# The end of a two-branch spectral kernel: last rows sent through DRAM, eight products without a reader, three pools with one buffer more, and a rewritten order

## The chip, the cores and the metric

The kernel runs on one core of a Trainium2 chip. The metric is device time in microseconds: the median of several executions, 537.49 us before the change. One more execution was profiled, and all durations below come from it.

## The reference

The input `x` is a float32 array of 2048 rows (positions) by 640 columns (channels). Two branches are computed from it and mixed by a gate per row:

```
g = sigmoid((x * gate_w).sum(-1))                      # one number per row
a: K[d, l] = 2 Re sum_n C[d, n] exp(A[d, n] dt[d] l)   # 128 complex modes per channel
   y = irfft(rfft(x, 4096) * rfft(K, 4096))[:2048] + x * D_skip
b: y = irfft2(rfft2(x) * (w_r + 1j * w_i))
out = g * a + (1 - g) * b
```

Branch a is a causal convolution along the 2048 positions with a generated filter K. Branch b is a filter in the two-dimensional spectrum.

## The kernel before

Everything is float32 except the arguments of the exponentials, which are split into bfloat16 parts. A Fourier transform of length 4096 is done as two stages of matrix products (`stage1`, 64x128 outputs, and `stage2`, 64x160 outputs) with tables that come in as inputs. The 640 channels are worked in four chunks of 160, called `c`, and the 4096 frequencies in 17 pairs of blocks, gathered in groups that start at block pair `g0`.

The program has these parts:

- `phase_p` prepares the parameters of the modes. `phase_a`, first half, transforms `x` and writes its spectrum to DRAM (`u_d`). `phase_b` generates the filter K: exponentials and sines on ScalarE (`e`, `sc`), their products on VectorE and GpSimd (`x`, `y`), outer products on TensorE (`p_k`, L745), result to DRAM (`k_d`).
- `phase_a`, second half, is branch b: for each of nine block pairs it folds the spectrum (`fo`, `fg`), transposes it on TensorE (`p_t`), copies that to `ft` on ScalarE (L555), multiplies with tables (`p_d`, L566 and L567), filters on VectorE (`mm`, `zz`, `pm`, `ff`), transposes back (`p_t`, copied to `pmt`, L553), multiplies again (`p_eo`, L611 and L612) and writes `s3e_d` to DRAM. `ft` and `pmt` have one buffer each (pools `f_t` and `f_p`). This half runs interleaved with `phase_b`.
- `phase_c` and `phase_d` finish branch a. For each chunk: `stage1` and `stage2` on the filter (L367, L380), product with the stored spectrum `us` on VectorE (`ma` L856, `mb` L857) and sums on VectorE and GpSimd (`t2`, L862), inverse `stage2` (`p_i`, L886), a copy on ScalarE (`s3`, L888), and a write of `s3` to DRAM (`s3_d`, L898). `us` comes from pool `c_u`, three buffers, loaded on ScalarE's DMA queue (L843).
- The end of `phase_d` mixes: `last_e` multiplies the rows of branch b (`t3e`, product `p_e`, L172) and scales them with the gate (`oe`, L944); `last_c` does the same for branch a (`t3`, product `p_c`, L960), scales (L965) and adds (L966), or both in one instruction for the last chunk (L963). Each is called for two halves of eight rows (`a`), in three pieces of 3, 3 and 2 rows. `p_e` and `p_c` share a pool of two PSUM buffers.

The last chunk, c = 3, takes its groups in the order g0 = 0, 4, 8, 16, 12. `t3` of this chunk collects 64 rows from `s3` of groups 0, 4, 8 and 12. Groups 0, 4 and 8 go through DRAM like all others. Group 12 is the last work of the inverse transform; its rows go straight from `s3` to `t3` inside SBUF, by eight DMAs of 80 KB, four issued by SyncE (SP) and four by ScalarE (ACT), each into four partitions of `t3` (L896).

The order of all instructions on all five engines is written out as numbers: a table `ORDER` of index ranges per engine, and a table `CROSS` of extra edges between engines for buffers, put on the traced instructions by `arrange`.

Of the kernel before, what the change touches and what calls it, by code (L numbers as in the profile page):

```python
# [384 lines left out]
def phase_a(tc, A, T):  # L385
    nc = tc.nc
# [96 lines left out]
    with ExitStack() as ctx:  # L483
# [4 lines left out]
        wu, wo, wg, ac, wt, w3p, wb = pool("f_u", 1), pool("f_o", 1), pool("f_g", 1), pool("f_c", 1), pool("f_t", 1), pool("f_3", 2), pool("f_b", 1)  # L488
        wp, ww, w4, wk = pool("f_p", 1), pool("f_w", 1), pool("f_4", 3), pool("f_k", 2)
# [297 lines left out]
def phase_c(tc, A, T, ctx):  # L787
# [8 lines left out]
    T.kp, T.cc, T.up = pool("c_k", 2), pool("c_c", 1), pool("c_u", 3)  # L796
# [30 lines left out]
def phase_d(tc, A, T, ctx, out):  # L827
# [45 lines left out]
    def backs(c, g0, gn, st):  # L873
        t2 = st.t2
        if c == 3 and g0 in (4, 12):
            s3 = T.kp.tile([128, 20, 64], F32, tag="k", name="s3").rearrange("p q a -> p (q a)").rearrange("p (x d) -> p x d", d=160)
        else:
            s3 = w2k.tile([128, 8 if gn > 1 else 1, 160], F32, tag="s3%d" % min(2, gn), name="s3")
        np_ = gn * st.nl // 64
        k0 = 2 * g0  # L880
        for h in range(0, np_, 4):
# [9 lines left out]
            if k0 == 32:  # L891
                nc.scalar.dma_start(T.s3_d[c, 33], s3[0:64, 0, :])
            elif (c, g0) == (3, 12):
                t3 = t3s[3].rearrange("p x a d -> p (x a) d")
                for i in range(h, h + 4):
                    (nc.scalar if i % 2 else nc.sync).dma_start(t3[16 * i + 3:16 * i + 16:4], s3[:, i, :])  # L896
            elif h:
                nc.scalar.dma_start(T.s3_d[c, 2 * k0:2 * (k0 + h) + 8].rearrange("(x k) a d -> (k a) x d", k=2), s3[:, 0:h + 4, :])  # L898
# [28 lines left out]
    def load_c(c, p, n, eng=nc.sync):  # L927

        if p == 0 and c != 2:
            t3s[c] = dk.tile([128, 2, 16, 160], F32, tag="t3", name="t3")  # L930
        elif p == 0:
            t3s[c] = T.tp[0].tile([128, 32, 160], F32, tag="t1", name="t3").rearrange("p (x a) d -> p x a d", x=2)
        for y in range(p // 16, (p + n) // 16):
            src = T.s3_d[c, 16 * y:16 * y + 16].rearrange("k (j x a) d -> (k j) x a d", x=2, j=2)
            eng.dma_start(t3s[c][y::4], src)
# [77 lines left out]
    load_c(3, 32, 16, eng=nc.scalar)  # L1013
    run(last_c(2, 0))
    run(last_c(2, AG))
    for dst, ot in held:
# [121 lines left out]
```

## Time and profile before

| | |
|---|---|
| median of 3 runs | 537.49 us (534.48 to 539.0) |
| the profiled execution | 538.59 us |
| its span, first to last instruction | 536.8 us |
| mean granted TensorE clock | 0.975 |
| busy: TensorE | 496.7 us (93%) |
| busy: VectorE | 429.3 us (80%) |
| busy: ScalarE | 309.5 us (58%) |
| busy: GpSimd | 276.3 us (51%) |
| DMA | 99.89 MB, mean 186 GB/s |

TensorE is PE in the profile (matmuls) and PEld (weight loads), VectorE is DVE, ScalarE ACT, GpSimd POOL, SyncE SP. A float32 product shows as two matmuls in the trace, so eight products are 16 of its rows. "Clock" is the share of full speed that TensorE was granted. The 1.8 us between the profiled time and its span lie around the program.

### The profile page before, as it was taken

What the parts mean: (1) busy time and instruction counts of PE and PEld (TensorE: products, weight loads), DVE (VectorE), ACT (ScalarE), POOL (GpSimd) and SP (SyncE); (2) the same over time, 40 slices, a digit from 0 to 9 for tenths busy, and PEclk for the clock granted to TensorE, in tenths of its full rate; (3) what the DMA queues carried; (4) which work ended last, traced back from release to release, by engine and by line L of the source; (5) the groups of instructions that cost most, each with busy time, mean ns of one, the idle gap of its engine ahead of it and who ended that gap; (6) DMA issues with size and microseconds to landing.
All of it is one profiled execution on the core that took longest, in us unless ns stands there. A gap on an engine that the chain in (4) does not pass through costs nothing. (4 is left out here: it accounts for less than half of the span.)

```text
span 536.8 us, 17117 instructions
## 1 busy us (share of the span) xinstructions
PE 496.7 (93%) x7432; PEld 382.1 (71%) x7432; DVE 429.3 (80%) x644; ACT 309.5 (58%) x469; POOL 276.3 (51%) x285
## 2 busy tenths in 40 slices
PE   8889999989899999999999999889989999998945
PEld 6889976757566767767767676558958889987611
DVE  3699867887989999988979779553986987979933
ACT  4667065698686876876986977876313333341200
POOL 4596415466438275257264255163733666638740
PEclk9979999999879999999999999999999999999987
DMA  8927760582160433170512231284849799899962
GB/s 333 406 95 272 250 237 18 208 270 89 52 217 2 127 104 93 33 263 6 142 37 84 74 123 57 74 313 146 318 139 376 263 363 341 275 295 295 324 227 101
DMA packets 47666, 99.89 MB, mean 186 GB/s; under 512 B 3588, under 2 KB 33048, under 8 KB 45928
## 3 DMA queue, kind: packets, MB, share of 16 engines
q1 hardware_dynamic: 25544, 67.08, 36.3%
q10 hardware_dynamic: 19552, 22.19, 12.8%
q0 software_dynamic: 2496, 9.54, 5.2%
q8 instruction: 58, 0.95, 0.7%
q14 instruction: 16, 0.13, 0.1%
HBM read 59.47 MB, written 38.99 MB: 183 GB/s over the span
## 5 line engine op out<-in xcount | busy, mean ns | idle before, releaser
L380 PE MATMUL p_s<-t,w 128*64 128x160 f32 x1056 | 89.2, 307 | 4.4 <-ACT ut L415 3.6
L380 PEld LDWEIGHTS p_s<-t,w 128*64 128x64 f32 x1056 | 76.2, 135 | 13.0 <-ACT ut L415 4.2
L731 POOL TENSOR_TENSOR y<-e,sc 128x512 f32<-128x512 f32 x40 | 52.5, 1315 | 38.3 <-ACT sc L712 37.3
L706 PE MATMUL p_p<-rp,par 64*128 64x512 bf16 x480 | 62.6, 381 | 7.5 <-DVE x L728 6.2
L697 ACT ACTIVATE e<-p_e 128x1024 f32<-128x1024 f32 (+1 forms) x80 | 62.0, 815 | 8.7 <-PE p_e L696 7.5
L732 POOL TENSOR_TENSOR y<-e,sc 128x512 f32<-128x512 f32 x40 | 52.8, 1319 | 18.4 <-ACT sc L712 18.3
L718 ACT ACTIVATE p_p<-p_p 128x1024 f32<-128x1024 f32 x40 | 40.5, 1012 | 24.2 <-PE p_p L706 19.9
L368 ACT COPY t<-p_s 128x512 f32<-128x512 f32 x40 | 25.1, 628 | 46.8 <-PE p_s L367 41.1
L726 DVE SCALAR_TENSOR_TENSOR x<-e,p_p 128x512 f32<-128x512 f32 x40 | 27.3, 682 | 26.9 <-ACT p_p L718 26.9
L728 DVE TENSOR_TENSOR x<-e,p_p 128x1024 f32<-128x1024 f32 x40 | 48.5, 1213 | 0.0
L745 PEld LDWEIGHTS p_k<-x,y 128*32 128x32 f32 x2560 | 38.5, 111 | 14.0 <-issue 11.4
L888 ACT COPY s<-p_i 128x640 f32<-128x640 f32 x32 | 22.1, 693 | 43.9 <-PE p_i L886 36.7
L745 PE MATMUL p_k<-x,y 128*32 128x64 f32 x2560 | 44.7, 223 | 1.2 <-DVE x L728 0.5
L712 ACT ACTIVATE sc<-p_p 128x1024 f32<-128x1024 f32 x40 | 40.9, 1023 | 7.8 <-PE p_p L706 7.5
L862 POOL TENSOR_TENSOR t<-ma 64x320 f32<-64x320 f32 x32 | 29.4, 918 | 31.2 <-DVE ma L856 29.4
L886 PE MATMUL p_i<-t,w 128*64 128x160 f32 x528 | 42.6, 300 | 2.1 <-DVE mb L857 2.1
L706 PEld LDWEIGHTS <-par 64*128 64x128 bf16 x480 | 20.2, 94 | 33.0 <-issue 11.1
L367 PE MATMUL p_s<-c,kt 128*64 128x128 f32 x640 | 42.9, 273 | 0.0
L886 PEld LDWEIGHTS p_i<-t,w 128*64 128x64 f32 x528 | 37.3, 137 | 6.2 <-POOL t L862 1.6
L367 PE MATMUL p_s<-c,u 128*64 128x128 f32 x640 | 40.3, 283 | 1.0 <-DMA c<-in_t_c 1.0
L367 PEld LDWEIGHTS p_s<-c,u 128*64 128x64 f32 x640 | 37.5, 142 | 4.0 <-issue 3.4
L367 PEld LDWEIGHTS p_s<-c,kt 128*64 128x64 f32 x640 | 38.4, 136 | 1.6 <-POOL kt L807 0.4
(163 smaller groups left out, 1071.5 us busy)
## 6 DMA issues: line engine op xcount, KB each, us to landing
u_d<-ut SPq DMA_DIRECT2D x32, 320.0 KB
us<-u_d ACTq DMA_DIRECT2D x16, 640.0 KB
s_d<-s ACTq DMA_DIRECT2D x15, 640.0 KB
t<-s_d SPq DMA_DIRECT2D x14, 640.0 KB
ww<-in_w_l SPq DMA_DIRECT2D x8, 642.0 KB
ue<-u_d SPq DMA_DIRECT2D x8, 640.0 KB
k_d<-kt SPq DMA_DIRECT2D x4, 1280.0 KB
kt<-k_d SPq DMA_DIRECT2D x8, 640.0 KB
```

Of the source, the lines that this page charges most:

```text
L367: nc.tensor.matmul(p[64 * ri:64 * ri + 64, j, :], src(i + j), e1[ri], start=True, stop=True)
L380: ins = nc.tensor.matmul(p[64 * j:64 * j + 64, i, 160 * ri:160 * ri + 160], w2[:, x, 64 * ri:64 * ri + 64], t1[:, x // 2 if x < 32 else K0 ...
L697: st.exp = S.activation(ef[:, :, c:c + n], p[:, :, 0:n], AF.Exp)
L706: P.matmul(p[:, j, 0:n], pars[0][t][x], w[x, y:y + n], start=i == 0, stop=i == 2)
L712: S.activation(sc.rearrange("p d v i -> p (d v i)"), p.rearrange("p j w -> p (j w)"), AF.Sin, scale=TWO_PI)
L718: T.trig = st.trig = S.activation(f, f, AF.Sin, scale=TWO_PI)
L728: V.tensor_tensor(out=x[:, 0].rearrange("p d (h j) -> p d h j", h=2), in0=e[:, :, 0:64].rearrange("p d (h j) -> p d h j", h=2), in1=cx.uns ...
L731: G.tensor_tensor(out=y[:, 1], in0=e[:, :, 64:96], in1=sc[:, 0], op=ALU.mult)
L732: G.tensor_tensor(out=y[:, 0], in0=e[:, :, 64:96], in1=sc[:, 1], op=ALU.mult)
L745: P.matmul(st.pb[32 * r:32 * r + 32, o, :], y[:, ri, 4 * qq + JR[r], :], x[:, ri, 4 * qq + JR[r], :], start=t % 2 + qq + 1 - ri == 0, stop ...
L862: return eng.tensor_tensor(out=t2[64 * im:64 * im + 64, o, :], in0=m[l, :hn, 0, :], in1=m[l, :hn, 1, :], op=ALU.add if im else ALU.subtract)
L886: T.mm = P.matmul(p[x:x + 64, i // 2, 160 * (i % 2):160 * (i % 2) + 160], T.w3[:, k0 + h + i, x:x + 64], t2[:, h + i, :], start=True, stop ...
```

## The change

It has five parts.

1. Group 12 of the last chunk is written to `s3_d` like the others, in two DMAs of 320 KB on ACT, one after each copy of `s3`. Two new DMAs of 320 KB on SP read it back into `t3`, each for eight of 16 rows per partition (`load_c(3, 48, 16, 2)`). The eight 80 KB DMAs inside SBUF are gone.
2. Eight products of `s3` with itself (128x128 weights, 480 columns) go into a PSUM tile that nobody reads.
3. Pools `f_t` and `f_p` get two buffers.
4. Pool `c_u` gets four buffers.
5. The tables `ORDER` and `CROSS` are rewritten for all five engines.

The diff without the tables:

```
-        ... pool("f_t", 1), pool("f_3", 2), pool("f_b", 1)
-        wp, ww, w4, wk = pool("f_p", 1), ...
+        ... pool("f_t", 2), pool("f_3", 2), pool("f_b", 1)
+        wp, ww, w4, wk = pool("f_p", 2), ...
...
-    T.kp, T.cc, T.up = pool("c_k", 2), pool("c_c", 1), pool("c_u", 3)
+    T.kp, T.cc, T.up = pool("c_k", 2), pool("c_c", 1), pool("c_u", 4)
...
+        T.s3 = s3
...
-            elif (c, g0) == (3, 12):
-                t3 = t3s[3].rearrange("p x a d -> p (x a) d")
-                for i in range(h, h + 4):
-                    (nc.scalar if i % 2 else nc.sync).dma_start(t3[16 * i + 3:16 * i + 16:4], s3[:, i, :])
-            elif h:
-                nc.scalar.dma_start(T.s3_d[c, 2 * k0:2 * (k0 + h) + 8]..., s3[:, 0:h + 4, :])
+            elif h or (c, g0) == (3, 12):
+                x = h if (c, g0) == (3, 12) else 0
+                T.sd = nc.scalar.dma_start(T.s3_d[c, 2 * (k0 + x):2 * (k0 + h) + 8]..., s3[:, x:h + 4, :])
...
-    def load_c(c, p, n, eng=nc.sync):
+    def load_c(c, p, n, parts=1, eng=nc.sync):
...
+        w = 16 // parts
         for y in range(p // 16, (p + n) // 16):
             src = T.s3_d[c, 16 * y:16 * y + 16].rearrange("k (j x a) d -> (k j) x a d", x=2, j=2)
-            eng.dma_start(t3s[c][y::4], src)
+            for a in range(0, 16, w):
+                T.ld = eng.dma_start(t3s[c][y::4, :, a:a + w], src[:, :, a:a + w])
...
     load_c(3, 32, 16, eng=nc.scalar)
+    load_c(3, 48, 16, 2)
     run(last_c(2, 0))
     run(last_c(2, AG))
+    p = ps.tile([128, 2, 512], F32, tag="ps", name="p_w2")
+    for _ in range(8):
+        P.matmul(p[:, 0, 0:480], T.s3[:, 4, 0:128], T.s3[:, 5:8, :], start=True, stop=True)
     for dst, ot in held:
         nc.sync.dma_start(dst, ot[:, :, :])
```

What the tables decide at the program's end is best seen in the order itself. On TensorE, before, from the first inverse product of group 12 (`p_i_7044`) to the end of the program; `t_6810` is `t3` of chunk 2 and `t_6893` that of chunk 3:

```order
L886 MATMUL p_i_7044<-t_7002,w_5241 64x160 x8
L172 MATMUL p_e<-t3e,c_66 64x480 x4
L172 MATMUL p_e<-t3e,c_66 64x320 x2
L886 MATMUL p_i_7058<-t_7002,w_5241 64x160 x8
L960 MATMUL p_c<-t_6810,c_66 64x480 x4
L960 MATMUL p_c<-t_6810,c_66 64x320 x2
L960 MATMUL p_c<-t_6810,c_66 64x480 x4
L960 MATMUL p_c<-t_6810,c_66 64x320 x2
L960 MATMUL p_c<-t_6893,c_66 64x480 x4
```

On TensorE after the change, the same stretch (lines have moved by a few numbers; L1019 are the eight new products):

```order
L887 MATMUL p_i_7044<-t_7002,w_5241 64x160 x8
L172 MATMUL p_e<-t3e,c_66 64x480 x2
L172 MATMUL p_e<-t3e,c_66 64x320 x2
L887 MATMUL p_i_7055<-t_7002,w_5241 64x160 x8
L172 MATMUL p_e<-t3e,c_66 64x480 x4
L1019 MATMUL p_w_7101<-s_7043 128x480 x8
L172 MATMUL p_e<-t3e,c_66 64x320 x2
L960 MATMUL p_c<-t_6810,c_66 64x480 x4
L960 MATMUL p_c<-t_6810,c_66 64x320 x2
L960 MATMUL p_c<-t_6810,c_66 64x480 x4
L960 MATMUL p_c<-t_6810,c_66 64x320 x2
L960 MATMUL p_c<-t_6893,c_66 64x480 x4
```

The second half of `p_e` has moved behind the last inverse product, and the eight new products stand between its pieces, ahead of all `p_c` of chunks 2 and 3.

On ACT before, from the copy and write of group 16 (`s_7037`) to the end; `s_7043` is group 12:

```order
L890 COPY s_7037<-p_i_7038 128x160
L892 DMA s_d<-s_7037 64x160
L888 COPY s_7043<-p_i_7044 128x640
L896 DMA t_6893<-s_7043 4x32x160 x2
L935 DMA t_6893<-s_d 32x5120
L888 COPY s_7043<-p_i_7058 128x640
L896 DMA t_6893<-s_7043 4x32x160 x2
```

On ACT after, the same stretch:

```order
L891 COPY s_7037<-p_i_7038 128x160
L889 COPY s_7043<-p_i_7044 128x640
L896 DMA s_d<-s_7043 128x4x160
L893 DMA s_d<-s_7037 64x160
L889 COPY s_7043<-p_i_7055 128x640
L896 DMA s_d<-s_7043 128x4x160
L935 DMA t_6893<-s_d 32x5120
```

The load of rows 32 to 47 of `t3` (L935), which waits for the write of group 16, stood ahead of the second copy and now stands behind it.

On SP before, the last DMAs:

```order
L935 DMA t_6893<-s_d 32x5120 x2
L896 DMA t_6893<-s_7043 4x32x160 x4
L1017 DMA out<-ot 128x1280 x2
L971 DMA out<-ot 128x1280
L971 DMA out<-ot 128x960
```

On SP after:

```order
L935 DMA t_6893<-s_d 32x5120 x2
L935 DMA t_6893<-s_d 32x2x1280 x2
L1021 DMA out<-ot 128x1280 x2
L971 DMA out<-ot 128x1280
L971 DMA out<-ot 128x960
```

The two reads of group 12 stand where the four DMAs inside SBUF stood, ahead of the outputs of chunk 2.

More of the change, by code (lines that the diff above doesn't have):

```diff
@@ L485, in pool @@
             return ctx.enter_context(tc.tile_pool(name=name, side="right", reuse_waits="tile", bufs=bufs))
-        wu, wo, wg, ac, wt, w3p, wb = pool("f_u", 1), pool("f_o", 1), pool("f_g", 1), pool("f_c", 1), pool("f_t", 1), pool("f_3", 2), pool("f_b", 1)
-        wp, ww, w4, wk = pool("f_p", 1), pool("f_w", 1), pool("f_4", 3), pool("f_k", 2)
+        wu, wo, wg, ac, wt, w3p, wb = pool("f_u", 1), pool("f_o", 1), pool("f_g", 1), pool("f_c", 1), pool("f_t", 2), pool("f_3", 2), pool("f_b", 1)
+        wp, ww, w4, wk = pool("f_p", 2), pool("f_w", 1), pool("f_4", 3), pool("f_k", 2)
         ps = ctx.enter_context(tc.tile_pool(name="f_ps", side="right", reuse_waits="tile", bufs=3, space=PSUM))
@@ L1041 @@
     "PE": """
[22 rows of a table removed]
[23 rows of a table added]
 """,
     "DVE": """
[12 rows of a table removed]
[12 rows of a table added]
 """,
     "Activation": """
[10 rows of a table removed]
[10 rows of a table added]
 """,
     "Pool": """
[5 rows of a table removed]
[6 rows of a table added]
 """,
     "SP": """
[3 rows of a table removed]
+1+3 8+3 0 4+2 11 6+2 15+2 12 14 13 26 17+9 27 37 28+9 38+8 58 61 47 46 57 48+2 59 50+3 62 53+3 60 65 56 63 69 67 74 66 71 64 72 79 70 85 76 68 77 75
+81 90 83 73 82 80 87 78 88 95 86 92 84 93 91 89 97+3 96 94 100+2 106 108 107 102 104 103 105 109 112 111 113 110 116 115 114 118 117 124 122 120+2 119
+125 123 127 126 128+9
 """,
@@ L1111 @@
 P259>V591 P259>V595 P259>V596 P263>V601 P263>V602 P263>V606 P263>V607 P267>V612 P67>V169 P67>V174 P81>V208 P81>V210 P93>V241 P93>V243 S118>A477
-S118>A478 S119>A487 S119>A488 S119>A490 S119>A491 S119>A492 V143>P63 V143>P64 V143>P66 V147>P71 V147>P72 V147>P74 V161>P67 V167>P86 V167>P87 V167>P89
-V194>P81 V203>P100 V203>P101 V203>P103 V224>P93 V236>P109 V236>P110 V236>P112 V263>P108 V269>P127 V269>P128 V269>P130 V296>P122 V305>P141 V305>P142
-V305>P144 V329>P136 V338>P150 V338>P151 V338>P153 V365>P149 V398>P163 V427>P172 V485>P206 V485>P207 V485>P208 V485>P209 V529>P233 V529>P234 V529>P235
-V529>P236 V576>P259 V576>P260 V576>P261 V576>P262 V612>P272 V612>P273 V612>P274 V612>P275
+S118>A478 S119>A490 V143>P63 V143>P64 V143>P66 V147>P71 V147>P72 V147>P74 V161>P67 V167>P86 V167>P87 V167>P89 V194>P81 V203>P100 V203>P101 V203>P103
+V224>P93 V236>P109 V236>P110 V236>P112 V263>P108 V269>P127 V269>P128 V269>P130 V296>P122 V305>P141 V305>P142 V305>P144 V329>P136 V338>P150 V338>P151
+V338>P153 V365>P149 V398>P163 V427>P172 V485>P206 V485>P207 V485>P208 V485>P209 V529>P233 V529>P234 V529>P235 V529>P236 V576>P259 V576>P260 V576>P261
+V576>P262 V612>P272 V612>P273 V612>P274 V612>P275
 """
```

2 lines of the change are left out of this document (1 added, 1 removed), and 103 rows, old and new, of the table ORDER.

## The prediction

> **What bounds the kernel now.** I read the page first: busy shares and slices.
>
> ```profile
> PE 496.7 (93%) x7432; PEld 382.1 (71%) x7432; DVE 429.3 (80%) x644; ACT 309.5 (58%) x469; POOL 276.3 (51%) x285
> PE   8889999989899999999999999889989999998945
> PEclk9979999999879999999999999999999999999987
> ```
>
> TensorE is busy in nearly every slice, with VectorE close behind; only the last two slices (510 to 537 us) fall to 4 and 5 tenths, and there the granted clock falls too. So a change can win in two places: small waits spread over the first 510 us, or the end. The spread part comes from a table of stretches (columns: length, then busy time and count of each engine, clock, DMA share, GB/s):
>
> ```profile
> 125.00:150.00 25.00, 21.22 (x364) 14.89 (x365) 22.74 (x32) 17.85 (x24) 13.04 (x13) 0.89 0.25 79
> 275.00:300.00 25.00, 24.95 (x345) 18.17 (x342) 24.86 (x38) 18.16 (x28) 14.78 (x15) 1.00 0.22 66
> 450.00:475.00 25.00, 25.00 (x361) 23.99 (x358) 22.84 (x35) 9.86 (x16) 14.00 (x16) 1.00 0.87 285
> 100.00:375.00 275.00, 261.63 (x4028) 186.80 (x4028) 229.72 (x342) 214.48 (x313) 136.88 (x141) 0.98 0.36 117
> ```
>
> Between 100 and 375 us TensorE idles 13.4 of 275 us; the worst stretch, 125 to 150, has 3.8 of them and a clock of 0.89. In the next two rows nothing is left. There is little to win before the end.
>
> The end, first TensorE's own timeline, then the chain that ended last:
>
> ```profile
> 509.98 1.26 PE L886 MATMUL p_i<-t,w 128*64 128x160 f32 x16
> 511.06 5.09 PE L960 MATMUL p_c<-t,c 128*64 128x480 f32 x24
> 524.62 6.80 PE L960 MATMUL p_c<-t,c 128*64 128x480 f32 x20 [8.47 <-DMA out<-ot]
> ...
> 518.64 5.75 DMA out<-ot
> ```
>
> The last inverse product ends at 511.24. The mix of chunk 2 follows until 516.15, then TensorE stands still for 8.47 us. The profile names an output DMA as what ended the wait, but `p_c` of chunk 3 reads `t3`, not `ot`. What it can wait for is the last rows' DMAs:
>
> ```profile
> 512.16 0.53 ACTq L935 DMA_DIRECT2D t<-s_d  x1
> 512.74 0.69 ACT L888 COPY s<-p_i 128x640 f32<-128x640 f32 x1 [4.90 <-DMA s_d<-s]
> 513.46 1.51 ACTq L896 DMA_DIRECT2D t<-s  x2
> 516.23 2.76 SPq L1017 DMA_DIRECT2D out<-ot  x2
> ...
> 518.00:520.00 2.00, 0.00 (x0) 0.00 (x0) 0.00 (x0) 0.00 (x0) 0.62 (x1) 0.94 0.80 287
> 522.00:524.00 2.00, 0.00 (x0) 0.00 (x0) 0.00 (x0) 0.00 (x0) 0.00 (x0) 0.50 0.24 95
> 528.00:530.00 2.00, 1.92 (x8) 0.44 (x6) 1.64 (x5) 0.00 (x0) 0.00 (x0) 0.50 0.00 0
> ```
>
> ACT's second copy of group 12 could have run at 511.5, but stood 4.90 us behind the load L935, which waited for group 16's write. The small DMAs went out only at 513.46, and their data moved beside two outputs until 524, in the end at 95 GB/s with a quarter of the DMA engines at work. The clock column shows the rest of the damage: with TensorE empty it fell just before 520 and still stood at 0.50 up to 530, so nearly all of chunk 3's products ran at half clock.
>
> **The change part by part.** All sums are against the profiled execution: span 536.8 us, 538.59 with what lies around it, which is 1.10 above the median of 537.49.
>
> *Last rows through DRAM.* The copy no longer waits behind L935, and its write is issued about 1 us after the last inverse product (0.69 for the copy and the steps to it). The two DRAM steps are not in this trace in this form. The nearest rows:
>
> ```profile
> s3e_d<-s POOLq DMA_DIRECT2D x4, 320.0 KB, 2.8
> par<-par_d POOLq DMA_DIRECT2D x8, 160.0 KB, 2.9
> ...
> 382.45 8.89 DMA t3e<-s3e_d
> 397.82 10.23 DMA s_d<-s
> ```
>
> From below, a 320 KB write at 2.8 and a read at 2.9 make 5.7 us. From above, a 640 KB write and a 1280 KB read in the crowded start of the last phase make 10.23 + 8.89 = 19.1 us. The new transfers are small, and the outputs of chunk 2 are now queued behind them on SP instead of running beside them, so I stay near the lower end and take 8 us: `t3` is whole 9 us after the last inverse product.
>
> What TensorE has to do meanwhile, from the same point: the second half of `p_e`, which used to stand ahead of it, the eight products, then `p_c` of chunk 2.
>
> *Eight products.* Each is two passes of 480 columns with 128x128 weights. Two rows of full-width float32 products bound a pass:
>
> ```profile
> 1.44 3.41 PE L411 MATMUL p_w<-lg 128*128 128x512 f32 x4 [1.44 <-DVE lg L406]
> 1.00:4.30 3.30, 2.86 (x4) 1.17 (x4) 0.56 (x2) 1.28 (x1) 1.78 (x3) 1.00 0.74 230
> ...
> 339.74 1.08 PE p_i L626 x4
> 450.18 0.81 PE p_e L172 x4
> ```
>
> From above, the first four passes of the program: 0.85 for 512 columns, 0.80 for 480, so 12.8 us for 16. From below, L626 in the middle of the program: 0.27 for 320 columns, 0.40 for 480, so 16 x 0.40 = **6.4 us**. I take this one: the same width, float32, in steady work. (The last row, narrow products two side by side, gives 0.20 a pass, 3.2 us, but a full-width pass cannot share the array.)
>
> The Trainium skill speaks to the upper row: its page "TensorE: Matmul & The Clock Gate", section "Part 1: The HAM clock gate", says that TensorE begins at half rate and is released after about 3.4 us of work. By that rule the first row is a half-clock price, and 0.40 is right from both sides; the clock column shows 1.00 there, and by it the sum would be 6.4 us worse.
>
> The eight wait for the second copy, 0.9 us after the last inverse product; `p_e` covers that. So from there: `p_e` of half a chunk 2.2 us (two pieces of 0.81, one of two thirds of it), 6.4, then 5.1 for `p_c` of chunk 2. That is 13.7 us, and the data were there at 9. **Chunk 3 starts on TensorE's time, not on the DMA's.** The wait of 8.47 us goes, and 6.4 us of products stand in its place, in front of all that is left, so they cost their full length. The `p_e` moved behind is no cost, since it is missing ahead; VectorE's `oe` (L944) moves with it and runs beside the eight products.
>
> *The clock.* TensorE no longer stops, so chunk 3 runs at full clock. Before:
>
> ```profile
> 528.13 1.74 DVE L963 SCALAR_TENSOR_TENSOR ot<-p_c,gate,oe 128x160 f32<-128x160 f32 x5 [0.63 <-PE p_c L960]
> 530.66 2.59 DVE L963 SCALAR_TENSOR_TENSOR ot<-p_c,gate,oe 128x160 f32<-128x160 f32 x8 [0.79 <-PE p_c L960]
> 516.72 0.84 DVE L966 TENSOR_TENSOR ot<-ot,oe 128x320 f32<-128x320 f32 x1
> ```
>
> From 524.62 to the last L963 at 533.25 it took 8.63 us. At full clock VectorE sets the pace: a first product of 0.81, sixteen L963 of 2.59/8 = 0.32 (5.2 us), some 0.5 of seams, and about half of chunk 2's last add (0.84), which now stands directly ahead: 6.9 to 7.3. Gain **1.5 us**.
>
> *Buffers and order.* One buffer each for `ft` and `pmt` cost TensorE 0.3 and 0.7 us:
>
> ```profile
> PE p_eo L611 <- ACT pmt L553: 0.7, 1, 0.7
> PE p_d L566 <- ACT ft L555: 0.3, 1, 0.3
> DVE ma L856 <- issue: 6.3, 6, 3.4
> 391.39 2.55 PE L172 MATMUL p_e<-t3e,c 128*64 128x480 f32 x12 [2.39 <-DMA t3e<-s3e_d]
> ```
>
> Two buffers can give that 1.0 back. The third row includes VectorE's waits for `us`; most of it lies where TensorE is full, so a fourth buffer brings nothing I can name, and its earlier loads run beside reads that TensorE waits for, such as `t3e` in the last row. From -1.0 to +2.4, I take -0.5 for all of it: both waits sit in a place with other work.
>
> Sum: -8.47 + 6.4 - 1.5 - 0.5 = **-4.1 us**, that is 534.5 for an execution like the profiled one and **533.4** for the median.
>
> **Rivals.**
>
> *The order also fills waits* in the middle. For it: the 13.4 us of idle, and the low clock at 125 to 150. Against it: VectorE is at 22.7 to 24.9 of 25 in the quoted rows there. Half of it back is -6.7 more: 527. Chance 0.22.
>
> *Nothing net.* The order is another one on every engine, and a stall of 2 to 3 us can bring a half clock of its own:
>
> ```profile
> 29.01 2.13 PE L380 MATMUL p_s<-t,w 128*64 128x160 f32 x11 [2.71 <-ACT ut L415]
> 25.00:50.00 25.00, 22.25 (x358) 21.07 (x360) 24.69 (x20) 16.75 (x32) 23.17 (x15) 0.86 0.50 174
> ```
>
> A clock of 0.86 over 25 us is 7 us at half speed, 3.5 lost. One more such place eats the 4.1; so do products at 0.80 a pass (+6.4, 540). 536 to 540, say 538. This is also the case in which the change doesn't do what it says: a new wait at the end as long as the old one. Chance 0.22.
>
> *Slower: the trip through DRAM is late.* If write and read take what the upper rows say, 19.1 us, `t3` is whole 20.1 us after the last inverse product, TensorE waits 20.1 - 13.7 = 6.4 us, the clock falls again, and chunk 3 takes 8.63. Against 13.4 to the start of chunk 3 today (511.24 to 524.62) and 2.2 of `p_e` moved behind, that is 20.1 - 13.4 - 2.2 = +4.5 us, and +1 for outputs that end later: 543. It decides from a trip of 12.7 us on (13.7 less the 1.0 to the write). Against it: the transfers are a half and a quarter of those sizes, and the DMA share in 522 to 524 is 0.24. Chance 0.08.
>
> By the same section of that page a wait keeps the clock if it is shorter than some 3.4 us, and the trace agrees (stopped at 516.15, halved just before 520). By that rule this rival would pay for the clock only from a trip of 16.1 us on.
>
> *The forecast*, the end as summed and little else: 0.48.
>
> **How the numbers follow.** The forecast's own range is 530 to 537: the buffers and order by -0.5 to +2.9, `p_e` and seams by 1.5 either way, and runs of before lay from 534.5 to 539 around their median. To hold 8 in 10 the range takes in most of the case below it and of the one without gain: 526.5 to 540.5. A measurement of this kernel can tell about 1% (5.4 us), so faster begins at 532.1. Faster: 0.20 of the second case and 0.15 of the forecast, 0.35. Slower than 542.9: the late trip, 0.08. The rest, 0.57, is within 1%.
>
> **What would show it.** No wait of TensorE over 1 us behind the last inverse product, and none put down to a DMA ahead of chunk 3; the L1019 row at 16 passes and 6.4 us; clock 1.0 to the last product; sixteen L963 of 0.32 without a wait near 9 us; from the last inverse product to the end of the span 23.5 to 24.5 us instead of 25.6. It is wrong if chunk 3 still waits for a DMA, if L1019 takes under 5 or over 8 us, or if the last inverse product moves by more than 3.5 us beyond the 2.2 that `p_e` accounts for.

## The result, and the profile after

| | before | after |
|---|---|---|
| median | 537.44 us of 20 (534.1 to 539.81) | **542.07 us** of 20 (537.24 to 545.97) |
| ratio, 95% interval | | **1.008** [1.0056, 1.0104] |
| the profiled execution's span | 536.8 us | 541.2 us |
| last inverse product ends | 511.24 | 517.12 |
| from there to the end of the span | 25.6 us | 24.1 us |

The change costs 4.3 us; 533.4 was forecast, with a range up to 540.5. Medians hold every execution; ratios leave out those that the comparison counts as disturbed (2 of 20 here, five of twelve in e9, four of twelve in e12), so that a median can lie higher than its ratio. A ratio is turned into microseconds below with 537.4.

The page of after, busy time and slices:

```profile
PE 503.1 (93%) x7448; PEld 386.9 (71%) x7448; DVE 434.7 (80%) x644; ACT 308.4 (57%) x469; POOL 274.3 (51%) x285
PE   6989899979789989999999999988999999998896
PEclk8999999997978999999999999999999999999999
```

The hole at the end (4 and 5 before) is now 9 and 6, and the clock there is full. In exchange there are new 7s for TensorE in slices 9 and 11 (108 to 122 and 135 to 149 us), a clock of 7, 7 and 8 in slices 10, 12 and 13 right behind them (before has 8 and 7 in slices 11 and 12), and a first slice of 6 where there was 8. TensorE's timeline at the end of after, then one row of stretches of 2 us (the clock is the third number from the end):

```profile
515.86 1.26 PE L887 MATMUL p_i<-t,w 128*64 128x160 f32 x16
518.66 6.71 PE L1019 MATMUL p_w<-s 128*128 128x480 f32 x16
525.89 6.97 PE L960 MATMUL p_c<-t,c 128*64 128x480 f32 x32
533.37 2.66 PE L960 MATMUL p_c<-t,c 128*64 128x320 f32 x12 [0.52 <-DVE ot L963]
536.38 0.76 PE L960 MATMUL p_c<-t,c 128*64 128x320 f32 x4 [0.35 <-DVE ot L963]
...
536.00:538.00 2.00, 0.79 (x5) 0.23 (x4) 1.78 (x6) 0.00 (x0) 0.00 (x0) 1.00 0.76 308
```

This is the end that the prediction described: no wait of 8.47 us, the products in its place, full clock, 24.1 us from the last inverse product on. But it begins at 517.12, when 509 was expected. The loss lies ahead of it. TensorE's longer waits there, and three stretches of 25 us:

```profile
9.13 6.23 PE L367 MATMUL p_s<-c,u 128*64 128x128 f32 x80 [3.91 <-DMA c<-in_t_c]
122.04 1.94 PE L550 MATMUL p_t<-c,fg 128*128 128x128 f32 x8 [3.52 <-DVE ut L415]
149.19 0.82 PE L696 MATMUL p_e<-rm,par 48*128 48x256 bf16 x4 [2.24 <-ACT e L697]
192.46 0.53 PE L745 MATMUL p_k<-x,y 128*32 128x64 f32 x21 [1.09 <-issue]
494.01 1.03 PE L960 MATMUL p_c<-t,c 128*64 128x480 f32 x4 [2.07 <-issue]
...
0.00:25.00 25.00, 19.61 (x296) 16.43 (x298) 9.99 (x23) 10.24 (x19) 7.19 (x11) 0.93 0.90 339
100.00:125.00 25.00, 20.81 (x318) 13.89 (x316) 19.96 (x35) 16.74 (x21) 10.38 (x13) 0.94 0.73 249
150.00:175.00 25.00, 22.98 (x311) 16.23 (x312) 24.21 (x36) 16.96 (x26) 12.37 (x13) 0.81 0.38 133
```

"issue" means that the profile shows nothing that TensorE waited for. Which of these waits cost time, and whether the order or the buffers made them, the experiments had to tell.

### The profile page after: what moved, and what is told of

It is laid out like the page before. It is cut to its first block, busy times and chain, and to the rows that moved or that the text cites. A ratio compares the mean times of both kernels' runs of the same rounds, so it can differ in the third digit from the quotient of the medians.

```text
span 541.2 us, 17137 instructions
## 1 busy us (share of the span) xinstructions
PE 503.1 (93%) x7448; PEld 386.9 (71%) x7448; DVE 434.7 (80%) x644; ACT 308.4 (57%) x469; POOL 274.3 (51%) x285
## 4 chain that ended last, share of the span: by engine, by line
PE 58%; DVE 7%; ACT 4%; issue 2%; DVEq 0%; ACTq 0%
PE p_s L380 7%; PE p_p L706 6%; PE p_s L367 6%; PE p_i L887 6%; PE p_k L745 5%; PE p_i L626 4%; PE p_eo L611 3%; PE p_t L550 3%; PE p_d L566 3%; PE p_eo L612 3%; PE p_e L172 3%; PE p_c L960 3%; PE p_d L567 2%; PE p_e L696 2%; PE p_w L1019 1%
## 5 line engine op out<-in xcount | busy, mean ns | idle before, releaser
L380 PE MATMUL p_s<-t,w 128*64 128x160 f32 x1056 | 87.8, 305 | 2.7 <-ACT ut L415 1.2
L380 PEld LDWEIGHTS p_s<-t,w 128*64 128x64 f32 x1056 | 75.7, 135 | 12.1 <-issue 3.8
L731 POOL TENSOR_TENSOR y<-e,sc 128x512 f32<-128x512 f32 x40 | 54.9, 1374 | 28.4 <-ACT sc L712 28.4
L706 PE MATMUL p_p<-rp,par 64*128 64x512 bf16 x480 | 62.6, 385 | 4.1 <-ACT e L697 1.7
L732 POOL TENSOR_TENSOR y<-e,sc 128x512 f32<-128x512 f32 x40 | 53.6, 1339 | 24.1 <-ACT sc L712 20.2
L745 PE MATMUL p_k<-x,y 128*32 128x64 f32 x2560 | 46.5, 225 | 3.3 <-issue 3.1
L706 PEld LDWEIGHTS <-par 64*128 64x128 bf16 x480 | 20.8, 94 | 30.4 <-issue 12.1
```

The lines of the kernel that those rows point to most:

```text
L380: ins = nc.tensor.matmul(p[64 * j:64 * j + 64, i, 160 * ri:160 * ri + 160], w2[:, x, 64 * ri:64 * ri + 64], t1[:, x // 2 if x < 32 else K0 ...
L706: P.matmul(p[:, j, 0:n], pars[0][t][x], w[x, y:y + n], start=i == 0, stop=i == 2)
L731: G.tensor_tensor(out=y[:, 1], in0=e[:, :, 64:96], in1=sc[:, 0], op=ALU.mult)
L732: G.tensor_tensor(out=y[:, 0], in0=e[:, :, 64:96], in1=sc[:, 1], op=ALU.mult)
L745: P.matmul(st.pb[32 * r:32 * r + 32, o, :], y[:, ri, 4 * qq + JR[r], :], x[:, ri, 4 * qq + JR[r], :], start=t % 2 + qq + 1 - ri == 0, stop ...
```

## The experiments

All ratios are against before, run on the same chip beside them.

| run | what it is | ratio, 95% interval | median, us |
|---|---|---|---|
| e1_tail | before + new tail | 0.9995 [0.9968, 1.0022] | 536.57 |
| e2_tail_noprod | e1 without the products | 0.9874 [0.9843, 0.9905] | 530.36 |
| e3_order | new order and buffers, old tail | 1.0155 [1.0114, 1.0197] | 545.31 |
| e4_bufs | before + buffers | 1.0111 [1.0068, 1.0154] | 542.33 |
| e5_h96 | after, order of before up to 96 us | 1.015 [1.0101, 1.0199] | 546.17 |
| e6_h165 | the same up to 165 us | 1.0034 [1.0004, 1.0065] | 539.07 |
| e7_h340 | the same up to 340 us | 1.0001 [0.9972, 1.003] | 537.12 |
| e8_fold | after, one copy moved | 1.0118 [1.0078, 1.0159] | 542.83 |
| e9_fold2 | after, fold pair moved | 1.005 [1.0003, 1.0097] | 543.7 |
| e10_fold2_pk | e9, one block of p_k moved | 0.999 [0.9962, 1.0019] | 537.21 |
| e11_bufs_load | e4, one load moved | 0.9981 [0.9953, 1.001] | 536.52 |
| e12_after_noprod | after without the products | 1.0088 [1.0049, 1.0128] | 544.51 |
| e13_after | after again | 1.0121 [1.0068, 1.0174] | 547.08 |
| e14_pk | after, block of p_k moved | 1.0012 [0.9977, 1.0047] | 538.97 |
| e15_mend_noprod | e10 without the products | 0.9957 [0.9926, 0.9989] | 535.29 |
| e16_dense | before, block of p_k moved the other way | 1.0042 [1.0014, 1.007] | 540.06 |
| e17_pe_ahead | e1, p_e where it was | 0.9954 [0.9924, 0.9984] | 534.22 |
| e18_pe_ahead_noprod | e17 without the products | **0.985** [0.9804, 0.9896] | **529.62** |

### Tail, order and buffers apart

e1 is before with parts 1 and 2 of the change and only the last entries of the orders new; e2 leaves the eight products out, so nothing of the result.

```diff
 PE:  p_i group 12, first half
-     p_e x6
      p_i group 12, second half
+     p_e x4, (e1: eight products,) p_e x2
      p_c of chunk 2, p_c of chunk 3
```

> The order and the buffers of before up to the last group, then only the new tail: last rows through DRAM, half of p_e behind the last inverse product, the eight products. Theory 1 (the new tail is worth what the prediction summed, and the rewritten order of the rest ate it): 3 to 4.5 us under before, 533 to 534.5, with the last inverse product 2 us earlier than before (509 to 509.5) and no wait over 1 us behind it. Theory 2 (the new tail itself brings nothing, the loss is in it): 537 to 543, with a new wait behind the last inverse product.

> As the run before, without the eight products that nobody reads. Theory 1a (they stand in front of everything left and cost their length, less the wait that comes in their place): the last rows are whole about 9 us after the last inverse product, p_e and chunk 2's mix take 7.3, so a wait of 1.5 to 3 us at full clock: 4 us faster than with them, 529 to 531. Theory 1b (they hold the clock): a wait of 3 us or more, the clock falls and chunk 3 takes 8.6 us instead of 7: within 2 us of the kernel with them. Theory 2 (nothing in the tail matters): same as before.

TensorE's timeline of e1, and two stretches of 2 us (the clock again third from the end):

```profile
508.00 1.95 PE L887 MATMUL p_i<-t,w 128*64 128x160 f32 x16 [2.41 <-POOL t L862]
509.73 2.88 PE L172 MATMUL p_e<-t3e,c 128*64 128x480 f32 x8
...
508.00:510.00 2.00, 2.00 (x18) 1.86 (x20) 0.00 (x0) 0.01 (x1) 0.00 (x0) 0.63 0.83 235
510.00:512.00 2.00, 2.00 (x6) 0.49 (x4) 0.34 (x1) 0.69 (x1) 0.00 (x0) 0.52 0.56 189
```

The new tail brought 0.3 us, within the interval of nothing: a time between what the two theories named. The wait of 8.47 us is gone, but where `p_e` stood before, TensorE now waits 2.41 us for GpSimd's sums of the last group, and the clock falls to about half behind it (the same 16 passes of `p_i` take 1.26 at full clock, here 1.95). Without the products it is 6.5 us less (0.9995 to 0.9874), the time that theory 1a named (529 to 531), but without its wait of 1.5 to 3 us. In e2 TensorE has no wait ahead of chunk 3 at all: the three parts of `p_e` and chunk 2's mix, slowed by the same half clock, just last until the rows are there. TensorE's timeline of e2:

```profile
510.28 4.01 PE L172 MATMUL p_e<-t3e,c 128*64 128x480 f32 x12
514.27 7.01 PE L960 MATMUL p_c<-t,c 128*64 128x480 f32 x32
```

e3 is the opposite half: after with the old tail. e4 is before with the three `bufs` numbers alone.

> The order and the buffers of after up to the last group, and the old tail of before (small DMAs from SBUF to SBUF, no products). Theory 1 (the loss is in the rewritten order ahead of the tail): 8 us slower than before, 544 to 547, last inverse product at 518 to 520, and then 25.5 us as before. Theory 2 (the loss is in the tail): within 2 us of before.

> Before with two buffers for ft and pmt and a fourth for loads, its order untouched. If buffers alone matter: up to 1 us faster (the waits of 0.3 and 0.7 us behind ft and pmt go). If earlier loads collide with transfers that TensorE waits for: 2 us or more slower. Theory 1 as a whole expects no change, 536 to 538.

e3 is 8.3 us slower than before, as theory 1 had it, and its timeline of TensorE shows the old wait at the end again:

```profile
530.83 7.05 PE L960 MATMUL p_c<-t,c 128*64 128x480 f32 x20 [8.70 <-DMA out<-ot]
```

From e3 (1.0155) to after (1.008), which were not run side by side, the tail gains 4.0 us. So the loss is ahead of the tail. e4 was a surprise: the buffers alone cost 6.0 us, where "no change" was expected. ACT's timeline of e4, then TensorE's, then a stretch of 25 us:

```profile
350.45 0.34 ACTq L843 DMA_DIRECT2D us<-u_d  x1
350.81 1.28 ACT L712 ACT_TABLE_LOAD   x1 [3.65 <-PE p_eo L612]
...
353.18 1.46 PE L706 MATMUL p_p<-rp,par 64*128 64x512 bf16 x6 [2.83 <-ACT sc L712]
...
350.00:375.00 25.00, 19.89 (x345) 12.31 (x345) 10.58 (x14) 16.27 (x21) 13.52 (x13) 0.80 0.56 204
```

The second load of `us` stands in ACT's queue and goes out only at 350.45, when the last `p_eo` product has been made; before, it went out at 346.9. Behind it stand the phases (`sc`) that TensorE waits 2.83 us for, and the clock is at 0.80 over these 25 us, where before has 1.00. That a load waits for `p_eo` fits memory that now lies where `pmt` was; e11 (below) tests whether this one wait is the cost.

### The order of before up to a point in time

Three kernels take after, and on every engine the order of before for what before had started by a point in time; the rest follows in the order of after. Buffers and tail are those of after.

```
order[engine] = before[engine][:started by t]
              + [i for i in after[engine] if i is not among them]     # t = 96, 165, 340 us
```

> The changed kernel, but every engine's order up to 96 us is the one of before (what before had started by then, in before's order; all that is left follows in the order of after; buffers and tail of after). Theory A (the start costs: TensorE begins 3.2 us later, since the table it needs is issued half a microsecond later and behind larger loads): 4 to 5 us less than after, 537 to 538. Theory B (the start is made up by 40 us, where before has a stall of its own; the loss begins at 118 us): within 1 us of after, 541 to 543.

> As the run before, with the order of before up to 165 us. Theory B (the loss is made between 117 and 165 us, by VectorE's fold ahead of a copy that TensorE waits for, and the half clocks behind it): 5 to 7 us less than after, 535 to 537. Theory C (the loss is spread over the middle and the last phase): at most 2 us less, 540 to 542.

> As the run before, with the order of before up to 340 us. Theory B: as with 165 us, 534 to 537. Theory C: 2 to 4 us less than with 165 us. If loads placed for the fourth buffer must stand together with their own order ahead of 340 us: up to 5 us more than with 165 us, as with buffers alone.

e5 (1.015) is no faster than after, although its TensorE begins as early as before's: the late start of 3.2 us is made up, theory A falls. From e5 to e6 6.2 us go (1.015 to 1.0034), to a time between those of theories B and C; from e6 to e7 it is another 1.8, with intervals that overlap. With the order of before up to 340 us the kernel stands where e1 stands: the order behind 340 us costs nothing measurable.

### The wait behind the fold

The most visible wait of after is the 3.52 us at 118.5: VectorE's pair `fo` waits for a late load of `ue`, and behind it stands the copy that frees the PSUM buffer for `p_t`. e8 moves this copy, e9 the pair:

```diff
 DVE: L415 ut (last but one)
+     L415 ut (last)                           # e8, e9
-     L521 fo, L520 fo                         # e9
      L480 gate x4
-     L415 ut (last)                           # e8, e9
      L726 x, L727 x, L728 x
+     L521 fo, L520 fo                         # e9
```

> The changed kernel with one instruction of VectorE moved: the last copy of phase A (ut from p_s) stands ahead of the fold pair (fo from ue) instead of behind it. Theory B: the wait of 3.52 us at 118.5 and the half clock behind it go, 4 to 6 us less than after, 536 to 538. Rival: the wait only moves to the next thing that hangs on the late ue load, 0 to 2 us less, 540 to 542.

TensorE's timeline of e8 at 118 us, then at 190 us with a stretch of 6 us, and the same stretch of after:

```profile
121.56 0.62 PE L550 MATMUL p_t<-c,fg 128*65 128x128 f32 x4 [2.61 <-DVE gate L480]
123.92 1.41 PE L706 MATMUL p_p<-rp,par 64*128 64x512 bf16 x6 [1.74 <-DVE x L728]
...
188.05 0.86 PE L745 MATMUL p_k<-x,y 128*32 128x64 f32 x43
191.47 0.53 PE L745 MATMUL p_k<-x,y 128*32 128x64 f32 x21 [2.56 <-issue]
...
194.00:200.00 6.00, 6.00 (x28) 4.88 (x25) 2.08 (x4) 3.56 (x6) 0.00 (x0) 0.50 0.00 0
```

```profile
194.00:200.00 6.00, 5.59 (x44) 4.01 (x42) 4.12 (x8) 5.18 (x8) 1.03 (x3) 1.00 0.01 3
```

The wait only went to the next things behind the pair (the rival). And a second place came to light: a block of 64 `p_k` products breaks off after 43, and the other 21 come 2.56 us later, with nothing to wait for, and at half clock until past 200 us. After has the same break after the same 43 products, 1.09 us long and without the half clock.

### The break in p_k

The page of after lists among the DMA queues one that carries instructions: 58 packets, 0.95 MB, so 16 KB each.

```profile
q8 instruction: 58, 0.95, 0.7%
```

TensorE has 2 x 7448 products and weight loads, 257 to a packet. In three traces the break ends 1.3 to 1.4 us after a packet of this queue has landed (after: landed 191.02, on again 192.46; e8: 190.16 and 191.47; e13: 187.73 and 189.12). That gave theory F: three blocks of short products within 6 us use up the fetched instructions. e10 takes e9 and moves the third block:

```diff
 PE:  p_k, p_k (128 rows), p_eo and p_e
-     p_k (64 rows)
      p_eo, p_e and p_t for some 4 us
+     p_k (64 rows)
      p_p
```

> The changed kernel with VectorE's fold pair that waits for the late ue load moved behind all that TensorE waits for at 118 us: the last copy of phase A, the four gate copies and one set of x. Theory B (the wait there, in whatever part, and its half clock are the loss between 117 and 165 us): the waits of TensorE between 117 and 125 us sum to under 1.5 us instead of 3.8 to 4.4, 3 to 6 us less than after, 536 to 539. Rival (other waits of the same order take over, the loss is the order as a whole): 0 to 2 us less, 540 to 542.

> As the run before, and a third block of p_k products (64 short ones in 1.1 us), which follows two others within 6 us, moved some 6 us later. Theory F (TensorE's instructions are fetched in blocks of 16 KB and three such blocks use them up faster than they come, so it stands still there for 1.1 to 2.6 us without any wait, and in some executions falls to half clock behind it): the stop in the middle of p_k near 190 us goes, 1 to 4 us less than without this move. Rival (the stop comes from the DMAs beside it, not from the density of instructions): the stop only moves, within 1 us of the run before.

The executions of e9 lay between 536 and 550 us; its ratio of 1.005 against 1.0118 of e8 would give the fold pair some 3.7 us, but the two were not run side by side, and with this spread that is an estimate. e10 came to 0.999, beside e9 and on the same chip: 3.2 us less by the ratios, whose intervals overlap a little, 6.5 us less by the medians. Its executions lay between 535.6 and 541.1. Its third block runs through, in TensorE's timeline:

```profile
191.78 1.10 PE L745 MATMUL p_k<-x,y 128*32 128x64 f32 x64
```

e14 makes this move alone, beside the unaltered kernel (e13), and e16 makes the reverse move in before:

> The changed kernel again, unaltered, beside the three that follow, on the same chip: the base for them, since its executions lie 9 us apart. Theory F (the stop of TensorE in the middle of p_k at 191 us lasts 1 to 2.6 us by chance, and above some length brings a half clock): a spread of 7 us or more between its executions, median 541 to 545.

> The changed kernel with nothing but the third block of p_k moved some 6 us later. Theory F (this stop is the larger part of the loss): 3 to 5 us less than the changed kernel beside it, and a spread of its executions under 6 us. Theory B (the wait at 118 us behind the fold is the larger part, and both count alone): 1 to 2 us less, and the rest came in the earlier run from the fold.

> Before, untouched but for one move: the third block of p_k (64 products) goes 6.5 us earlier, where it stands in the changed kernel, 3 us behind the two others; by the trace its inputs are there by then. Theory F: a stop of 1 to 3 us in the middle of p_k with no releaser in the profile, in some executions with a half clock behind it: 1.5 to 7 us slower than before. Rival (the stop came from the DMAs of the changed order, not from the density of instructions): no such stop, within 1 us of before.

On that chip the unaltered kernel stood at 1.0121 with 540.3 to 549.9 us; its timeline of TensorE has the break, 2.02 us long, and a stretch of 4 us the half clock behind it:

```profile
189.12 0.86 PE L745 MATMUL p_k<-x,y 128*32 128x64 f32 x21 [2.02 <-issue]
190.00:194.00 4.00, 4.00 (x16) 2.82 (x17) 2.21 (x4) 2.11 (x3) 0.00 (x0) 0.50 0.03 7
```

e14 stands at 1.0012: this one block is worth 5.9 us, the larger part of the loss on that chip, although its spread (534.7 to 542.3) did not shrink below 6 us as theory F had it.

The traces suggest why a spread is left. After and e13 are the same program, but their traces lose time in different places. Count TensorE's `p_p` products (L706) in sets of twelve, in the order in which they start, and take how much later than in before a set begins:

| set of `p_p`, its begin in before | after | e13 | e14 | e10 |
|---|---|---|---|---|
| 7th, 116.3 us | 0.8 us | 1.6 | 0.9 | 1.0 |
| 8th, 123.0 us | 6.3 | 2.1 | 5.9 | 1.0 |
| 15th, 172.7 us | 6.9 | 2.6 | 4.8 | 1.4 |
| 16th, 190.9 us | 8.8 | 10.1 | 5.4 | 1.9 |

The trace of after loses 5.5 us at the wait behind the fold and the half clock that follows it, and only 1.9 at the break, which was short in that execution. The trace of e13 loses 0.5 us at the fold, where TensorE's wait was 0.56 us at full clock, and 7.5 at the break. The row of that wait and ten microseconds of e13, then the same ten of after:

```profile
119.85 1.06 PE L550 MATMUL p_t<-c,fg 128*128 128x128 f32 x8 [0.56 <-DVE ut L415]
120.00:130.00 10.00, 8.83 (x122) 6.78 (x123) 8.08 (x12) 8.50 (x13) 8.44 (x9) 1.00 0.40 141
```

```profile
120.00:130.00 10.00, 7.67 (x92) 5.38 (x92) 7.87 (x14) 5.60 (x8) 5.01 (x6) 0.66 0.32 108
```

e14 has no break left, but its trace still has the wait behind the fold, 3.51 us; e10, with both moves, has neither. So the fold is a second cause; how often it strikes, and what it costs in the median, was not measured.

But e16 contradicts the theory's simple form. It is 2.3 us slower than before, and its third block, as close to the others as in after, does not break (TensorE's timeline):

```profile
184.29 1.10 PE L745 MATMUL p_k<-x,y 128*32 128x64 f32 x64
```

So density alone does not make the break. The traces of all these runs give the second condition. Number TensorE's products and weight loads in the order in which they start. In every kernel that has the break it comes when 5,786 of them have started (5,787 in e6). Other stops with "issue", in `p_k` but for the first, come after 443, 3,244, 4,770, 8,843, some 10,877 and 11,133. From 443 on these numbers, 5,786 among them, are 11, 17, 21, 33, 41 and 42 times 254.5 away, to within 7: one packet of 16 KB each, if instructions that these rows do not count make up for the rest of its 257. Call 254.5 of them an instruction block. At 38 ends of such blocks, in 15 traces, TensorE paused for more than 0.6 us from one start to the next, and each time it went on 1.2 to 1.6 us after a packet of `q8` had landed (median 1.4). So it was, as far as the traces can tell, waiting for its instructions. (One pause is of another kind: after 696, in nine traces, before among them, where the packet had landed 3.6 us earlier or more.) The packet for the next instruction block lands some time after TensorE has begun the one before it (median 1.9 us in before, 2.1 in after), and that time decides. For the instruction block that ends at 5,786, worked out from the start of each instruction, the landing of each packet, and SyncE's timeline:

| kernel | its instructions take | load of `ue` issued, from the block's begin | packet landed, from the block's begin | break |
|---|---|---|---|---|
| before | 9.6 us | +4.1 us | 2.1 us | none |
| e16 | 4.2 | +4.1 | 1.9 | none |
| e14 | 9.8 | -1.15 | 3.9 | none |
| e10, e15 | 9.8 | -1.16, -1.14 | 4.7, 4.2 | none |
| e9, e6, after, e3 | 4.2 | -1.15, -0.9, -1.15, -1.14 | 4.13, 4.12, 4.09, 4.20 | 0.99, 1.07, 1.09, 1.19 us |
| e12, e13, e5, e8 | 4.2 | -1.14, -1.15, -1.15, -1.15 | 4.75, 5.06, 5.32, 5.69 | 1.81, 2.02, 2.27, 2.56 |

The length of the break is the time of the landing less 3.0, within 0.15 us. Two things have to meet: the instruction block runs in 4.2 us (the third block of `p_k` close behind the others), and its successor's packet comes after 4 us and more instead of 2. Before has neither, e16 only the first, e10, e14 and e15 only the second. The packet is late where a load of 640 KB (`ue`) went out about a microsecond ahead of the instruction block. After's timeline of SyncE and its DMA traffic from 187 to 191 us, then the row of SyncE in e16, whose instruction block begins at 180.71:

```profile
185.79 0.37 SPq L514 DMA_DIRECT2D ue<-u_d  x1
...
q1 hardware_dynamic: 528, 0.66, 49.3%
q0 software_dynamic: 36, 0.10, 7.9%
q8 instruction: 1, 0.02, 1.5%
```

```profile
184.85 0.37 SPq L514 DMA_DIRECT2D ue<-u_d  x1
```

In after the 0.66 MB of `ue` pass beside the one packet of instructions; in e16 the load goes out when the packet has long landed. That both are needed is shown by e14, which takes the instruction block of 4.2 us away and keeps the late packet, and e16, which has it alone; that `ue` is what delays the packet rests on the times alone, since no kernel moved that load by itself. Why the packet takes 4.1 us beside it in one trace and 5.7 in another stays open. e6 has the break and loses little: it is the long ones, with the half clock behind them, that cost. So a part of the 6.2 us between e5 and e6 may be the length of the break (2.27 and 1.07 us in their traces), and not the order from 96 to 165 us. The 2.07 us of after at 494 us are at no end of an instruction block; what TensorE waited for there stays open.

### One load in ACT's queue

e11 is e4 with one instruction moved, to about where the order of after has it:

```diff
 ACT: L843 us
-     L843 us
      L712 sc, L718 p_p, L615 o
+     L843 us
      L843 us
```

> Before with the buffers of after (two for ft and pmt, four for loads) as in the run with buffers alone, which was 5 us slower, and one instruction of ACT moved: the second load of us stands behind the copy of o (L615) instead of ahead of the table load. Theory L (with more buffers this load needs memory that pmt still holds, waits for p_eo in ACT's queue, and with it the phases that stand behind it): the 5 us come back, 536 to 538. Rival (the fourth buffer's loads disturb others): 540 to 542.

0.9981: all of the 6 us come back, theory L. In the order of after the loads stand behind `o` (L615), so this cost is not in after; it is what more buffers cost without a new order. Which of the three pools made the load wait was not taken apart.

### The products in the new order, and p_e by itself

e12 and e15 leave the eight products out of after and of e10.

> The changed kernel without the eight products. Theory T (in this order the last rows are whole only 12.4 us after the last inverse product, against 9.2 in the kernel without products on the order of before; TensorE has 7.4 us of other work, so the products mostly stand in a wait): a wait of about 5 us, half clock in chunk 3, within 2 us of after, 540 to 543. Theory P (they cost their length as they did on the order of before): 6 us less than after, 535 to 537.

> The changed kernel with both moves (fold pair behind what TensorE waits for, third block of p_k later), and without the eight products. In the trace of the changed kernel without products the end from the last inverse product on took 20.2 us instead of 24.1, behind a wait of 2.7 us at full clock. Theory T2 (products cost 4 us of their 6.7 also in this order, and the median without them was hidden by the stop at 190 us): 532.5 to 534. Theory T (they only fill a wait in this order): 536 to 538.

In the trace of e12 TensorE gets the rows for the first products of chunk 3, the first of the two reads, 10.2 us after the last inverse product (517.52), and waits for them (its timeline; the clock stays at 1.00 there):

```profile
527.76 1.83 PE L960 MATMUL p_c<-t,c 128*64 128x480 f32 x8 [2.73 <-DMA t<-s_d]
```

From the last inverse product the end takes 20.2 us there instead of 24.1, but the ratio, 1.0088, shows no gain over 1.008; the break in that run was long (1.81). From e10 to e15 the products are worth 1.8 us (0.999 to 0.9957), between the two theories, on two chips and with intervals that overlap. So in the new order they stand partly in a wait, and how much of 4 us they cost there is not settled. e17 and e18 are e1 and e2 with all of `p_e` back ahead of the last inverse product:

> The order and buffers of before up to the last group, last rows through DRAM and the eight products, as in the first run, but all of p_e stays ahead of the last inverse product. In the first run TensorE then waited 2.41 us there for POOL's t, with a half clock behind it, which p_e had covered. If the prediction's step 'the p_e moved behind is no cost' was wrong by that cover: no wait over 1 us ahead of the last inverse product, 2 to 3 us less than the first run, 533.5 to 535 (0.994 to 0.997 of before). If it was right: within 1 us of the first run.

> As the run before, without the eight products. The last rows are whole about 9.2 us after the last inverse product, and TensorE has only the 5.1 us of chunk 2's mix in between: a wait of 4 us. If it keeps the clock: 530 to 531.5. If the clock falls behind it, as it did behind the 8.47 us of before: 532 to 534. With p_e behind the last inverse product the same kernel took 530.4; theory P2 (late p_e is worth having only where no products fill the wait) expects this one to be slower than that by 0.5 to 3 us.

TensorE's timeline of e17, then of e18 with a stretch of 2 us:

```profile
515.57 6.71 PE L1019 MATMUL p_w<-s 128*128 128x480 f32 x16 [1.40 <-ACT s L889]
```

```profile
511.63 1.26 PE L887 MATMUL p_i<-t,w 128*64 128x160 f32 x16
519.89 1.83 PE L960 MATMUL p_c<-t,c 128*64 128x480 f32 x8 [2.08 <-DMA t<-s_d]
...
520.00:522.00 2.00, 1.72 (x8) 0.43 (x7) 1.05 (x4) 0.00 (x0) 0.28 (x1) 1.00 0.79 300
```

With `p_e` back, the wait of 2.41 us is gone and the new tail brings 2.5 us (0.9954); the products now wait 1.40 us for the copy that `p_e` had covered. Without them the first read is there 7.0 us after the last inverse product (512.89), the wait is 2.08 us and the clock holds: 0.985, the lowest ratio of all. e2 is at 0.9874, and the two intervals overlap, so theory P2 (e18 slower than e2) has no support.

## Why the prediction was wrong, by its own steps

*The wait of 8.47 us goes.* Right. In after nothing waits for a DMA ahead of chunk 3. The trip through DRAM was put at 8 us, `t3` whole 9 us after the last inverse product. That was too short: in after the second read landed at 529.49, 12.4 us after it (12.1 in e12, 9.4 in e18; the first read, where TensorE waited for it, was there after 10.2 and 7.0). It cost nothing, because chunk 3 began on TensorE's time, 13.9 us after the last inverse product where 13.7 were summed; the margin was 1.5 us and not 4.7.

*Eight products cost 6.4 us in full.* Right in size, 6.71 for the row, and on the order of before also in time: 6.5 us from e1 to e2, 5.6 from e17 to e18. Of the two rows that bounded a pass, the one from the middle of the program was the right one. In the order of after they seem to cost less than that, which is not settled.

*The clock holds in chunk 3.* Right: 1.00 to the end, sixteen L963 of 0.32 us, 24.1 us from the last inverse product where 23.5 to 24.5 were said. The three terms of the end sum to -3.6; e3 to after gives -4.0, e17 -2.5.

*The p_e moved behind is no cost, since it is missing ahead.* **Failed on the order of before.** What stood ahead was cover: GpSimd's sums end later than TensorE gets there, and without `p_e` TensorE waits 2.41 us and loses the clock. From e1 to e17 the move costs 2.2 us, as much as it seemed to bring, though on two chips and with intervals that overlap; the wait and the half clock are in the traces. The question that was asked of the stall (what is late next when it goes) was not asked of the work that was moved away.

*Buffers and order: -0.5, from -1.0 to +2.4.* **This is the step that failed.** It measured +8.3 us (e3). The two waits of 0.3 and 0.7 us and the loads were priced; a new order on five engines was given no price of its own, and its rows are read only at the end of the program. The loss sits in places that no duration of before shows: a break in the middle of `p_k`, for instructions that come late (5.9 us by e13 and e14), and the fold pair ahead of a copy (5.5 us in the trace of after, 0.5 in that of e13). On the order of before the buffers alone cost as much, by one load in ACT's queue (6 to 7 us, e4 and e11).

*The rivals.* "Nothing net" had the mechanism, a new stall of 2 to 3 us that brings a half clock, but priced one such place at 3.5 to 4.1 us, ending at 538; the run of after had several. "Late trip" came out at 543, near the time measured, by a mechanism that did not happen; that its number fits is luck. The prediction's rule that a wait under some 3.4 us keeps the clock did not hold: the half clock came behind waits of 1.8 to 2.6 us (below). The sign that would show it wrong (the last inverse product more than 3.5 us off the 2.2 of `p_e`) is the one that appeared: it came 5.9 us later, not 2.2 earlier.

## What to carry to other kernels

A rewritten order is a change to the whole program: its risk belongs in the range as a term of its own, bounded by what one stall of 2 to 3 us with a half clock costs here (about 6 us: 5.9 by e13 and e14, 6.0 in e4), even when only its end looks new. Look in a new order for some 250 short instructions of TensorE in a row beside a large load. Before moving work behind a milestone, ask what it covered where it stood. Filler products are worth their place only while the data are still away: take them out and look, since a wait of 2 us at full clock was cheaper here than 6.7 us of products.

## What the runs showed of the hardware

- TensorE can stop, as it seems for lack of instructions, in the middle of products whose inputs were there; the profile shows it only as "issue". In these traces the next 16 KB (254.5 counted instructions, an instruction block) land about 2 us after the block ahead has begun (medians of 1.9 in before and 2.1 in after), 3.1 to 6.3 us after it where a pause followed, and TensorE goes on 1.2 to 1.6 us after they have landed. An instruction block of short `p_k` products that runs in 4.2 us does not cover a packet that lands after 4 us and more. The Trainium skill, page "Runtime: NRT & Kernel Launch", section "Instruction fetch mechanics", has the same blocks of 16 KiB or 256 instructions, and says that the cost of crossing one's end is mostly hidden. The traces agree on the size; it was hidden at most ends of instruction blocks, and at 38 of them TensorE paused for 0.6 to 2.8 us from one start to the next.
- The half clock came behind waits much shorter than the 8.47 us of before: 1.81, 2.02, 2.27 and 2.56 us in `p_k`, 2.41 in e1. It did not come behind 2.08 us in e18 and 2.73 in e12. One wait of after's order, 2.24 us ahead of `p_e` (149.19 in after), stands in the traces of after, e13 and e14 with the same length: in after and e13 the half clock comes with its end, in e14 it doesn't. The Trainium skill, page "TensorE: Matmul & The Clock Gate", section "HAM oscillation — how this bites in real kernels", gives as an abstract rule that idle gaps of TensorE over some 3.4 us are to be avoided; here gaps of 1.8 to 2.6 us were already enough in five traces, so the measurement decides: not the length of one gap alone sets it.
- Larger pools made the kernel slower with nothing else changed: 6 us in e4, by one load that waited in ACT's queue and held up what stood behind it (e11). That it waited for memory that had become shared fits the trace, but no run shows it.
